# RWKV attention and a gated feed-forward network on one core: the first two chunks of two batches in 64-row half tiles of token pairs

## The chip, the core and the metric

The kernel runs on one core of a Trainium2 chip. It uses TensorE (PE in the profile; PEld is its weight loads), VectorE (DVE), ScalarE (ACT), GpSimd (POOL) and the DMA queues that SyncE (SP) and GpSimd issue. The metric is device time in microseconds, the median of several runs.

## What is computed

Inputs r, k, v, w are float32 of shape 4 batches x 8 heads x 768 tokens x 48. Each head keeps a 48x48 state; then a feed-forward network runs over all 3072 tokens, 384 wide, with 1536 units between:

```python
for t in range(S):
    cur = np.einsum('bhd,bhe->bhde', u[None] * kt, vt)
    y[:, :, t] = np.einsum('bhd,bhde->bhe', rt, state + cur)
    state = wt[:, :, :, None] * state + np.einsum('bhd,bhe->bhde', kt, vt)
...
x = y.transpose(0, 2, 1, 3).reshape(B * S, H * D)
xn = x / np.sqrt(np.mean(x * x, -1, keepdims=True) + 1e-6) * rms_g
g = xn @ w_gate
return (g / (1 + np.exp(-g)) * (xn @ w_val)) @ w_out
```

## The kernel before

The tokens of a batch are cut into 6 chunks of 128. A step is written `name.n.j`, for chunk n (0 to 5) of batch j (0 to 3). For each chunk:

- `load_r`, `load_k`, `load_v`, `load_w` (lines 256 to 271): a tile of 128 tokens by 8 heads by 48, in pieces of 192 bytes, because a head's row of one token is 48 floats. For the chunks in `WIN` (chunks 0 and 1 of each batch) one load of w brings 256 tokens, two tokens to a partition, in pieces of 384 bytes.
- `ln` (ACT) and `cs_mm` (PE): the logarithm of w and its running sums over the tokens, by matmuls with triangular masks. `exp_r`, `exp_k` (ACT) give the decays, `r_mul` (DVE) and `k_mul` (DVE or POOL) the decayed r and k, `w_tot` (DVE) the chunk's total decay.
- `rk_pe`, `rk_tr`: r and k are transposed, by PE and a copy in chunks 0 and 1, by a DMA transpose in later ones.
- `q_mm` (lines 493 to 504): the scores of a chunk, four pairs of heads, 48 rows by 128x128, even heads and odd heads in two banks. `q_mask_e`, `q_mask_o` mask them on DVE (or ACT and POOL).
- `st_mm`, `st_new`: the state's update. `y_mm` (lines 540 to 549): scores times v, 8 matmuls, and from chunk 1 on r times state, 4 matmuls.
- `bonus_mul`, `bonus_v` (POOL) and `bonus_sum` (DVE): the term with u. `x_add` (DVE) adds it to y; `x_sq`, `x_rstd`, `xn_mul` are the norm; `xn_pe` and `xn_out` (or a DMA transpose and `xn_gain`) give the transposed input of the network.

The network works on groups of 512 tokens (4 chunks). The table `COL` makes group 0 of chunks 0 and 1 of batches 0 and 1, and group 1 of those of batches 2 and 3. A group has 12 units of 128 columns: `gate_mm`, `val_mm` (line 617: three matmuls of 512 columns each; line 622: group 1, whose 512 tokens are done in two halves), `silu` (ACT), `h_mul` (DVE); then `o_mm` (line 660) for each chunk, `o_out` and `out_dma`. The weights come by `load_gv.g.h`: g 0 is the first 4 units, g 1 the other 8; h 0 is gate, h 1 value. `load_wo` brings the last matrix.

The order of all steps is written out by hand in the string `ORDER` (lines 25 to 126). Each engine takes its instructions in that order, SP its loads and POOL its weight loads too. PSUM has two banks in ring a, two in ring b and four in ring q. A step with `:m` in the table first does m filler matmuls with a tile of zeros into its bank (lines 235 to 241; three transposes for one filler where the bank is bfloat16). Sets such as `CAST_ACT`, `K_POOL`, `RK_DVE`, `ODD_DVE`, `RSTD_ACT`, `OUT_DVE` say which engine does a step for which chunk.

Of the kernel before, what the change touches and what calls it, by code (L numbers as in the profile page):

```python
# [30 lines left out]
bonus_mul.1.0 q_mask_e.0.0 load_k.1.3 load_r.1.2 load_k.1.2 load_r.1.3 load_v.1.2 bonus_mul.0.1 load_w.2.1 load_w.2.0
load_v.1.3 load_w.2.3 q_mm.1.0:2 cs_mm.1.1 exp_r.1.1 exp_k.1.1 r_mul.0.1 k_mul.0.1 w_tot.0.1 q_mask_o.1.0
bonus_sum.1.0 load_gv.0.1 cast_v.0.1 load_r.2.0 bonus_sum.0.1 r_mul.1.1 load_w.2.2 rk_pe.0.1:2 ln.0.3 y_mm.0.0
rk_tr.0.1 st_mm.0.1:4 x_add.0.0 q_mask_e.1.0 st_new.0.1 cs_mm.0.3:3 bonus_v.0.1 cast_v.1.0 q_mm.0.1:1 y_mm.1.0
k_mul.1.1 bonus_v.1.0 cast_v.1.1 q_copy_o.0.1 x_sq.0.0 bonus_mul.1.1 load_r.2.1 x_add.1.0 exp_r.0.3 load_r.2.2
x_sq.1.0 load_r.2.3 load_k.2.0 q_mask_e.0.1 w_tot.1.1 rk_pe.1.1:1 rk_tr.1.1 q_mm.1.1:7 q_mask_o.1.1 load_gv.0.0
q_mask_o.0.1 y_mm.0.1:8 g_mm.0.0 bonus_sum.1.1 ln.0.2 x_rstd.1.0 xn_mul.1.0 x_rstd.0.0 xn_mul.0.0 exp_k.0.3
bonus_v.1.1 load_gv.1.0 q_mask_e.1.1 x_add.0.1 x_sq.0.1 x_rstd.0.1 y_mm.1.1 x_add.1.1 k_mul.0.3 xn_pe.1.0:2 xn_pe.0.0
cs_mm.0.2 g_out.0.0 xn_out.1.0 x_sq.1.1 xn_mul.0.1 xn_out.0.0 r_mul.0.3 st_mm.1.1:3 x_rstd.1.1 st_mm.1.0 xn_mul.1.1
xn_pe.0.1 xn_out.0.1 w_tot.0.3 rk_pe.0.3:3 xn_pe.1.1 xn_out.1.1 exp_r.0.2 exp_k.0.2 r_mul.0.2 val_mm.0.0:4 gate_mm.0.3  # L40
silu.0.3 val_mm.0.3 rk_tr.0.3 w_tot.0.2 st_new.1.1 load_gv.1.1 k_mul.0.2 bonus_mul.0.2 q_mm.0.3 h_mul.0.3 st_new.1.0
gate_mm.0.2 gate_mm.0.0 rk_pe.0.2 silu.0.0 silu.0.2 val_mm.0.2 q_mask_e.0.3 h_mul.0.0 gate_mm.0.5 gate_mm.0.1 silu.0.5
silu.0.1 val_mm.0.1 rk_tr.0.2 q_copy_o.0.3 h_mul.0.1 bonus_mul.0.3 bonus_sum.0.3 h_mul.0.2 gate_mm.0.6:1
gate_mm.0.11:1 q_mm.0.2 cast_v.0.2 silu.0.6 silu.0.11 q_mask_o.0.2 gate_mm.0.8 val_mm.0.6 q_mask_e.0.2 cast_v.0.3
st_mm.0.2 val_mm.0.11 q_mask_o.0.3 h_mul.0.6 val_mm.0.5 y_mm.0.3 y_mm.0.2 bonus_sum.0.2 bonus_v.0.2 load_wo.0.0
# [668 lines left out]
```

## Time and profile before

| | |
|---|---|
| runs (3) | 203.38, 205.18, 205.36 us, median 205.18 |
| span of the profiled execution | 202.2 us; its own time isn't listed apart, the lowest run is 1.2 us above the span |
| first matmul of group 0 | 30.21 us |
| DMA, SP's queue | 119504 packets, 28.58 MB |

The page gives the busy time and share of each engine and a row of digits, each for a fortieth of the span (9 is 90% or more busy). In a timeline a row is the start, the length, the engine, the source line, the operation and its tiles, the number of instructions in it, and in brackets how long the engine stood idle before and what released it. Matmuls overlap: the time that one takes from the next is read from start to start.

### The profile page before, as it was taken

What the parts mean: (1) busy time and instruction counts of PE and PEld (TensorE: products, weight loads), DVE (VectorE), ACT (ScalarE), POOL (GpSimd) and SP (SyncE); (2) the same over time, 40 slices, a digit from 0 to 9 for tenths busy, and PEclk for the clock granted to TensorE, in tenths of its full rate; (3) what the DMA queues carried; (4) which work ended last, traced back from release to release, by engine and by line L of the source; (5) the groups of instructions that cost most, each with busy time, mean ns of one, the idle gap of its engine ahead of it and who ended that gap; (6) DMA issues with size and microseconds to landing.
All of it is one profiled execution on the core that took longest, in us unless ns stands there. A gap on an engine that the chain in (4) does not pass through costs nothing.

```text
span 202.2 us, 4604 instructions
## 1 busy us (share of the span) xinstructions
PE 191.3 (95%) x1677; PEld 121.9 (60%) x1694; DVE 157.5 (78%) x307; ACT 135.0 (67%) x278; POOL 124.4 (62%) x178
## 2 busy tenths in 40 slices
PE   1999799999999999999999998999999999999993
PEld 0566485565568998865556664656555555555562
DVE  6489789799989799997999998988989782225711
ACT  2637885779699657898678985899676683335310
POOL 6488959175769962689858556988699554200000
PEclk9999999999999999999999999999999999999999
DMA  6999999999999998989899999995464013030132
GB/s 144 231 234 207 212 208 202 195 179 208 206 184 225 160 212 191 210 185 188 199 176 215 237 188 203 183 190 108 134 179 104 0 23 99 0 117 0 63 115 99
DMA packets 121567, 32.42 MB, mean 160 GB/s; under 512 B 116420, under 2 KB 120392, under 8 KB 121544
## 3 DMA queue, kind: packets, MB, share of 16 engines
q1 hardware_dynamic: 119504, 28.58, 66.6%
q0 software_dynamic: 2032, 3.54, 9.9%
q8 instruction: 13, 0.21, 0.4%
q14 instruction: 10, 0.08, 0.1%
q10 hardware_dynamic: 8, 0.00, 0.0%
HBM read 25.96 MB, written 4.72 MB: 152 GB/s over the span
## 4 chain that ended last, share of the span: by engine, by line
PE 65%; ACT 3%; DMA 2%; DVE 2%; issue 1%; SPq 0%; DVEq 0%; ACTq 0%
PE ps_av L617 7%; PE ps_bu L617 7%; PE ps_au L617 7%; PE ps_bv L617 6%; PE ps_qx L660 6%; PE ps_qv L660 6%; PE ps_qu L660 5%; PE ps_qz L660 4%; PE ps_au L622 2%; PE ps_bu L622 2%; DMA rkT<-rk 2%; PE ps_av L622 2%; PE ps_bv L622 2%; ACT L249 1%; PE ps_au L419 1%; PE ps_qv L500 1%
## 5 line engine op out<-in xcount | busy, mean ns | idle before, releaser
L660 PEld LDWEIGHTS <-ht 128*128 128x128 bf16 x300 | 28.1, 98 | 17.5 <-DVE ht L646 1.0
L251 ACT ACTIVATE sg<-ps_av 128x512 bf16<-128x512 f32 x36 | 21.5, 597 | 22.8 <-PE ps_av L617 18.0
L646 DVE TENSOR_TENSOR ht<-ps_bv,sg 128x512 bf16<-128x512 f32 x29 | 19.9, 687 | 13.9 <-PE ps_bv L617 12.9
L251 ACT ACTIVATE sg<-ps_au 128x512 bf16<-128x512 f32 x36 | 21.5, 596 | 11.5 <-PE ps_au L617 7.7
L617 PEld LDWEIGHTS <-wg_sb 128*128 128x128 bf16 x180 | 19.2, 114 | 15.9 <-issue 0.6
L617 PEld LDWEIGHTS <-wv_sb 128*128 128x128 bf16 x180 | 19.2, 114 | 15.7 <-issue 0.5
L465 POOL TENSOR_TENSOR ruk<-rt,kt 128x384 f32<-128x384 f32 x24 | 24.0, 1001 | 3.7 <-DMA kt<-in_k_dram 2.8
L475 POOL TENSOR_TENSOR ydiag<-vt,diag 128x384 f32<-128x384 f32 x24 | 20.4, 859 | 9.4 <-DVE diag L470 9.1
L617 PE MATMUL ps_av<-xnt,wg_sb 128*128 128x512 bf16 x88 | 25.0, 381 | 0.3
L466 POOL TENSOR_TENSOR ruk<-ruk,u_bc 128x384 f32<-128x384 f32 x24 | 24.0, 1001 | 1.9
L617 PE MATMUL ps_bu<-xnt,wv_sb 128*128 128x512 bf16 x86 | 24.8, 380 | 0.4
L646 DVE TENSOR_TENSOR ht<-ps_bu,sg 128x512 bf16<-128x512 f32 x31 | 21.3, 686 | 4.8 <-PE ps_bu L617 3.1
L617 PE MATMUL ps_au<-xnt,wg_sb 128*128 128x512 bf16 x87 | 23.6, 380 | 0.1
L617 PE MATMUL ps_bv<-xnt,wv_sb 128*128 128x512 bf16 x82 | 23.2, 380 | 0.2
L459 POOL TENSOR_TENSOR rk<-kt,ek 128x384 bf16<-128x384 f32 x16 | 15.9, 1001 | 9.7 <-ACT ek L251 5.9
L249 ACT ACT_TABLE_LOAD x14 | 18.0, 1283 | 1.9 <-PEq L698 1.6
L660 PE MATMUL ps_qx<-wo_sb,ht 128*128 128x384 bf16 x96 | 17.1, 326 | 0.2 <-DVE ht L646 0.2
L558 ACT ACTIVATE junk<-xb 128x384 bf16<-128x384 f32 x24 | 12.5, 522 | 6.3 <-DVE xb L553 6.2
L571 ACT ACTIVATE xn<-xb,rstd 128x384 bf16<-128x384 f32 x24 | 14.2, 609 | 0.6 <-POOL rstd L567 0.5
L470 DVE TENSOR_REDUCE diag<-ruk 128x8 f32<-128x384 f32 x24 | 13.1, 544 | 1.9 <-POOL ruk L466 1.9
L660 PE MATMUL ps_qv<-wo_sb,ht 128*128 128x384 bf16 (+1 forms) x84 | 13.8, 314 | 0.0
L251 ACT ACTIVATE lw<-wt 128x384 bf16<-128x384 f32 (+1 forms) x20 | 11.6, 583 | 2.8 <-DMA wt<-in_w_dram 2.7
(170 smaller groups left out, 408.2 us busy)
## 6 DMA issues: line engine op xcount, KB each, us to landing
rt<-in_r_dram SPq DMA_DIRECT2D x24, 192.0 KB, 4.0
vt<-in_v_dram SPq DMA_DIRECT2D x24, 192.0 KB, 3.9
kt<-in_k_dram SPq DMA_DIRECT2D x24, 192.0 KB, 3.9
out_dram<-ob SPq DMA_DIRECT2D x23, 192.0 KB, 2.2
wt<-in_w_dram SPq DMA_DIRECT2D x16, 192.0 KB, 3.7
wt<-in_w_dram SPq DMA_DIRECT2D x4, 384.0 KB, 4.3
wo_sb<-in_moe_w_out_dram POOLq DMA_DIRECT2D x3, 384.0 KB, 7.3
wg_sb<-in_moe_w_gate_dram POOLq DMA_DIRECT2D x1, 768.0 KB, 9.2
```

What stands on the lines that cost most here:

```text
L249: nc.scalar.preload_act_table_set(table_name)
L251: return nc.scalar.activation(**kw).ins
L459: eng.tensor_tensor(out=rk[:, n % 2, j, 1, :, 0:D], in0=inp["k", n, j], in1=bank["cs_k", n, j][:, 0:DM].rearrange("p (h d) -> p h d", h=H) ...
L465: nc.gpsimd.tensor_tensor(out=ruk[n, j], in0=inp["r", n, j], in1=inp["k", n, j], op=ALU.mult)
L466: nc.gpsimd.tensor_tensor(out=ruk[n, j], in0=ruk[n, j], in1=u_bc, op=ALU.mult)
L470: nc.vector.tensor_reduce(out=diag[n, j].rearrange("p h o -> p (h o)"), in_=ruk[n, j], axis=mybir.AxisListType.X, op=ALU.add)
L475: nc.gpsimd.tensor_tensor(out=ydiag[n, j], in0=inp["v", n, j], in1=diag[n, j].to_broadcast([128, H, D]), op=ALU.mult)
L571: nc.scalar.activation(out=xn, in_=xb[n, j], func=AF.Copy, scale=rstd[n, j][:, 1:2])
L617: nc.tensor.matmul(ps, lhsT=units(ws, c, f), rhs=x[:, c, :], start=(c == 0), stop=(c == KC - 1))
L622: nc.tensor.matmul(ps[:, i * TS // 2:(i + 1) * TS // 2], lhsT=units(ws, c, f + i), rhs=x[:, c, cols], start=(i == 0 and c == 0), stop=(i = ...
L646: nc.vector.tensor_tensor(out=ht[n][:, f, :], in0=v, in1=sg, op=ALU.mult)
L660: nc.tensor.matmul(ps[:, cols], lhsT=ht[n][:, f, b * L:(b + 1) * L], rhs=wo_sb[:, f, cols], start=(f == 0), stop=(f == FC - 1))
```

## The change

Chunks 0 and 1 of batches 0 and 1 (the set `PAIR`) are laid out anew. A tile now holds one chunk of both batches: partitions 0 to 63 batch 0, 64 to 127 batch 1, each partition two neighbouring tokens. So r, k, v and w of one batch and chunk come as a 64-partition load in pieces of 384 bytes. A step `name.n.0` now means the even tokens of both batches, and `name.n.1` the odd ones. The sums use new masks `mp`, the scores new masks `mq`. Scores are 64x64 blocks for a batch: `q_mm` does 16 matmuls with 64 output rows in place of 8, `y_mm` 32 on scores in place of 8 and 8 on the state in place of 4, `st_mm` 8 in place of 4. The pair tiles lie in buffers that `ht` and `wo` use later. An output tile of such a chunk is written by two DMAs. The other batches keep the old form (`WIN` is now batches 2 and 3).

The sets that give steps to engines change, the order of all steps is new, and the new table has no filler. At its start it reads

```diff
-load_r.0.0 load_w.0.0 u_mm.0.0 ln.0.0 load_v.0.0 load_k.0.0 cs_mm.0.0:2 load_r.1.0 load_w.0.1 u_out.0.0 load_k.1.0
+u_mm.0.0 load_w.0.1 load_w.0.0 load_k.0.1 load_r.0.1 u_out.0.0 ln.0.0 cs_mm.0.0 load_w.1.0 load_r.0.0 load_k.0.0
```

The core of the rest:

```diff
-    CAST_ACT = sel("00 01 02 03 20 21 30 31 33 40 43 53")
+    CAST_ACT = sel("00 01 10 12 20 22 23 40 41 50 51 52 53")
-    K_POOL = sel("02 10 20 21 22 23 30 31 32 33 40 42 43 50 51 53")
+    K_POOL = sel("01 02 11 13 20 22 23 30 31 33 40 41 42 43 50 51 52")
-    WIN = sel("00 01 02 03 10 11 12 13")
+    WIN = sel("02 03 12 13")
+    PAIR = sel("00 01 10 11")
-    RK_DVE = sel("00 02 03 10 11 12 13")
-    ODD_DVE = sel("00 02 10 11 13 20 23 40 43 52")
-    RSTD_ACT = sel("00 10 11 13 20 32 33")
-    OUT_DVE = sel("00 01 10 13 20 21 22 30 33 40 42 50 52 53")
+    RK_DVE = sel("01 02 03 12 13")
+    ODD_DVE = sel("00 01 03 10 11 20 22 32 33 43 51")
+    RSTD_ACT = sel("00 01 03 11 12 13 21 43")
+    OUT_DVE = sel("00 03 11 22 31 40 42 50")
...
     def load(which, n, j):
         t = {"r": r, "k": k, "v": v}[which]
+        if (n, j) in PAIR:
+            if which == "v":
+                if "pv" not in inp:
+                    inp["pv"] = pt.tile([128, 2, H, 2, D], FP32, name="wo", bufs=1)
+                o = inp["pv"][:, n]
+            else:
+                if "prk" not in inp:
+                    inp["prk"] = pt.tile([128, 2, 2, H, 2, D], FP32, name="ht", bufs=NHT)
+                o = inp["prk"][:, n, "rk".index(which)]
+            b = j % 2
+            nc.sync.dma_start(out=o[b * PD:(b + 1) * PD].rearrange("p h i d -> p h (i d)"),
+                              in_=t[j, :, n * L:(n + 1) * L, :].rearrange("h (p i) d -> p h (i d)", i=2))
+            return
...
     def cs_mm(n, j):
+        if (n, j) in PAIR:
...
+            for x in range(2):
+                nc.tensor.matmul(o, lhsT=mp[:, int(x < i)], rhs=lw[:, n % 2, j0 + x, :, 0:D], start=(x == 0),
+                                 stop=(i == 1 and x == 1))
+            for q in range(0 if i else NP):
+                for x in range(2):
+                    nc.tensor.matmul(a[:, 2 * q:2 * q + 2], lhsT=pair(lw[:, n % 2, j0 + x], q), rhs=hb,
+                                     start=False, stop=(q == NP - 1 and x == 1))
...
     def q_mm(n, j):
+        if (n, j) in PAIR:
+            t, x = inp["rkT"][:, n], j % 2
...
+            for i in range(NP):
+                for b in range(2):
+                    at_b = slice(b * PD, (b + 1) * PD)
+                    for d0, o in ((0, qe), (PD, qo)):
+                        nc.tensor.matmul(o[at_b, i, :].rearrange("p (a x) -> p a x", a=2), lhsT=t[d0:d0 + D, NP + i, x, at_b],
+                                         rhs=t[d0:d0 + D, i, :, at_b], start=(i == 0), stop=(i == NP - 1))
...
     def y_mm(n, j):
+        if (n, j) in PAIR:
...
+            for h in range(H):
+                for s in range(2):
+                    for b in range(2):
+                        nc.tensor.matmul(ps[halves[b], h * D:(h + 1) * D],
+                                         lhsT=qts[n, j0 + s][halves[b], h % 2, h // 2, x * PD:(x + 1) * PD],
+                                         rhs=vb[n, j0 + s][halves[b], h, :], start=(n == 0 and h == 0 and s == 0),
+                                         stop=(h == H - 1 and s == 1))
...
     def out_dma(n, j):
+        if (i, j) in PAIR:
+            for b in range(2):
+                row0 = (j - j % 2 + b) * S + i * L
+                nc.sync.dma_start(out=out[row0:row0 + L].rearrange("(p a) m -> a p m", a=2)[j % 2],
+                                  in_=bank[ob][b * PD:(b + 1) * PD])
+            return
```

Three places of the order bear on the prediction. On PE, the last rows ahead of group 0. Before (L528 is `st_mm`, L586 `xn_pe`, L238 and L240 fillers, L482 `rk_pe`, L617 the network):

```order
L528 MATMUL ps_qu<-vb,rk 128x96
...
L586 MATMUL ps_qz<-ident,xn 128x128
...
L238 MATMUL ps_qv<-ident,zero 128x128
...
L482 MATMUL ps_qv<-ident,rk 128x128
...
L240 LDWEIGHTS zero
L240 MATMUL ps_bv<-zero 128x384
...
L617 LDWEIGHTS wv_sb_128
L617 MATMUL ps_bv<-xnt,wv_sb_128 128x512
```

The same place now (L711 is `xn_pe`, L633 `st_mm`, L553 `rk_pe`, L742 the network):

```order
L711 MATMUL ps_qv<-ident,xn 128x128
...
L633 LDWEIGHTS rk
L633 MATMUL ps_qu<-vb,rk 128x96
...
L553 LDWEIGHTS rk
L553 MATMUL ps_qv<-ident,rk 128x128
L742 LDWEIGHTS wg_sb_142
L742 MATMUL ps_au<-xnt,wg_sb_142 128x512
```

The fillers are gone, group 0 begins with a gate unit of the 8-unit part (`wg_sb_142`) where it began with a value unit of the 4-unit part (`wv_sb_128`), and `rk_pe` of both (0, 3) and (0, 2) stands ahead of it.

On POOL, the steps around the weight loads. Before (L465 and L466 are `bonus_mul`, L475 `bonus_v`, L389 `cast_v`, L351 the weights, L518 a mask, L566 and L567 `x_rstd`):

```order
L465 TENSOR_TENSOR ruk<-rt,kt 128x384
L466 TENSOR_TENSOR ruk<-ruk,u_bc 128x384
L351 DMA wv_sb_128<-in_moe_w_val_dram 128x3x512
L475 TENSOR_TENSOR ydiag<-vt,diag 128x384
L389 CAST vb<-vt 128x384
...
L351 DMA wg_sb_126<-in_moe_w_gate_dram 128x3x512
L518 AFFINE_SELECT qts<-qts 128x512
...
L351 DMA wg_sb_127<-in_moe_w_gate_dram 128x3x1024
L566 TENSOR_SCALAR rstd<-rstd 128x1
L567 TENSOR_TENSOR rstd<-rstd,mhalf 128x1
L351 DMA wv_sb_129<-in_moe_w_val_dram 128x3x1024
```

Now (L546 is `bonus_v`, L536 and L537 `bonus_mul.1.0`, L395 the weights, L435 `cast_v`, L530 `k_mul`, L691 and L692 `x_rstd`):

```order
L546 TENSOR_TENSOR ydiag<-wo,diag 128x384
L536 TENSOR_TENSOR ruk<-ht 128x384
L537 TENSOR_TENSOR ruk<-ruk,u_bc 128x384
L395 DMA wg_sb_142<-in_moe_w_gate_dram 128x3x1024
L395 DMA wv_sb_144<-in_moe_w_val_dram 128x3x1024
L435 CAST vb<-wo 128x384
L546 TENSOR_TENSOR ydiag<-wo,diag 128x384 x3
L530 TENSOR_TENSOR rk<-kt,ek 128x8x48
L691 TENSOR_SCALAR rstd<-rstd 128x1
L692 TENSOR_TENSOR rstd<-rstd,mhalf 128x1
L395 DMA wg_sb_141<-in_moe_w_gate_dram 128x3x512
L395 DMA wv_sb_143<-in_moe_w_val_dram 128x3x512
```

The two large weight loads now come first, behind all four `bonus_mul` and one `bonus_v`, and the small ones last.

On PE, the scores and `y_mm` of the first chunk, one matmul of each kind. Before:

```order
L500 LDWEIGHTS rkT
L500 MATMUL ps_qz<-rkT 128x128
L502 LDWEIGHTS rkT
L502 MATMUL ps_qu<-rkT 128x128
...
L548 LDWEIGHTS qts
L548 MATMUL ps_qz<-vb,qts 128x48
```

Now:

```order
L583 LDWEIGHTS ht
L583 MATMUL ps_qz<-ht 64x128
...
L583 MATMUL ps_qu<-ht 64x128
...
L662 LDWEIGHTS qts
L662 MATMUL ps_qu<-vb,qts 64x48
```

The outputs have 64 rows in place of 128, and there are 16 and 32 such matmuls in a step where there were 8 and 8.

More of the change, by code (lines that the diff above doesn't have):

```diff
@@ L31 @@
[L31 to L45, printed above, removed]
@@ new lines @@
+w_tot.1.3 r_mul.1.3 val_mm.0.1 gate_mm.0.0 silu.0.0 val_mm.0.2 y_mm.0.3 rk_pe.1.2 h_mul.0.2 gate_mm.0.1 silu.0.1
+val_mm.0.0 gate_mm.0.3 gate_mm.0.6 x_add.0.3 load_wo.0.0 k_mul.1.3 load_wo.1.0 x_rstd.0.2 load_wo.2.0 st_new.0.3
+h_mul.0.1 silu.0.3 x_sq.0.3 rk_tr.1.2 h_mul.0.0 xn_mul.0.2 silu.0.6 rk_pe.1.3 val_mm.0.3 q_mm.1.2 load_r.2.2 rk_tr.1.3
+cs_mm.2.1 val_mm.0.6 bonus_mul.1.2 bonus_mul.1.3 q_mask_e.1.2 h_mul.0.3 h_mul.0.6 cs_mm.2.0 q_mm.1.3 q_copy_o.1.2
+cast_v.1.2 x_rstd.0.3 q_mask_o.1.2 o_mm.0.2 bonus_sum.1.2 y_mm.1.2 bonus_v.1.2 q_mask_e.1.3 cs_add.2.0 ln.2.2
@@ L212, in banks_of @@
         }
+        if fn == "w_tot" and (n, j) in PAIR:
+            j -= j % 2
         return [(x, n, j) for x in found.get(fn, ())]
```

303 lines of the change are left out of this document (198 added, 105 removed).

## The prediction

> **What bounds the kernel now.** I read the page first, then the busy time by stretches, then the timeline of the first 30 us, and last the waits. Of the page, the totals, PE's row of the 40 slices and DMA's row:
>
> ```profile
> span 202.2 us, 4604 instructions
> ...
> PE 191.3 (95%) x1677; PEld 121.9 (60%) x1694; DVE 157.5 (78%) x307; ACT 135.0 (67%) x278; POOL 124.4 (62%) x178
> ...
> PE   1999799999999999999999998999999999999993
> ...
> DMA  6999999999999998989899999995464013030132
> ```
>
> PE is busy 95% of the span and the DMA engines are full for three quarters of it. The average hides two stages, so the next view cuts the span where the first matmul of the second network starts (the last columns are granted clock, DMA share and GB/s):
>
> ```profile
> 7.93:30.16 22.23, 20.44 (x269) 14.49 (x268) 18.49 (x40) 15.41 (x37) 17.58 (x23) 1.00 1.13 221
> 30.21:199.01 168.80, 167.02 (x1394) 105.72 (x1409) 135.04 (x256) 116.91 (x239) 102.63 (x141) 1.00 0.73 153
> ```
>
> From 30.21 us on, PE is idle 168.80 - 167.02 = 1.8 us in 169: the long stretch is PE's work and almost nothing else. Before it, in what I call the head, PE looks full too, but 70 of its matmuls there and just behind it are fillers with zeros (the counts on `zero`):
>
> ```profile
> L240 PEld LDWEIGHTS <-zero 128*128 128x128 bf16 x40 | 3.5, 98 | 2.8 <-issue 1.1
> ...
> L238 PEld LDWEIGHTS <-zero 128*128 128x128 bf16 x30 | 2.2, 107 | 0.5 <-issue 0.3
> ...
> 22.97 1.47 PE L240 MATMUL ps_qv<-zero 128*128 128x384 bf16 x8
> ```
>
> So the head is paced by others: DVE is busy 18.49 of 22.23 us, POOL 17.58. It ends with this chain, from the last chunk's sum through its norm and transpose to the first matmul of group 0:
>
> ```profile
> 7.93 0.56 DVE L453 TENSOR_TENSOR rk<-rt,ps_au 128x384 bf16<-128x384 f32 x1 [1.54 <-ACT ps_au L251]
> ...
> 25.92 0.56 DVE L553 TENSOR_TENSOR xb<-ps_qx,ydiag 128x384 f32<-128x384 f32 x1 [0.30 <-PE ps_qx L548]
> ...
> 28.50 0.62 ACT L571 ACTIVATE xn<-xb,rstd 128x384 bf16<-128x384 f32 x1
> ...
> 29.60 0.56 DVE L596 TENSOR_TENSOR xnt<-ps_qz,gT 128x384 bf16<-128x384 bf16 x1 [0.43 <-PE ps_qz L586]
> ...
> 30.21 0.81 PE L617 MATMUL ps_bv<-xnt,wv_sb 128*128 128x512 bf16 x2
> ```
>
> The time is therefore the moment of that first matmul, plus PE's work behind it, plus PE's stalls behind it, plus a tail of 3.2 us (202.2 - 199.0) that the change leaves alone.
>
> **The change, part by part.** *PE's work behind the first matmul.* The order shows the same 360 + 144 + 300 matmuls of the second network there, with the same shapes, and the same attention steps but two: the eight transposes of `rk_pe.0.2` are now ahead of it, and two fillers are gone. The eight transposes take 0.44 us from start to start:
>
> ```profile
> 28.79 0.61 PE L482 MATMUL ps_qv<-ident,rk 128*128 128x128 bf16 x8
> ...
> 29.23 0.33 PE L586 MATMUL ps_qz<-ident,xn 128*128 128x128 bf16 x3
> ...
> 36.94 0.33 PE L240 MATMUL ps_av<-zero 128*128 128x384 bf16 x1
> ...
> 37.10 0.81 PE L617 MATMUL ps_av<-xnt,wg_sb 128*128 128x512 bf16 x3
> ```
>
> A filler takes 0.16 us. Together -0.44 - 0.32 = **-0.8 us**. The fillers of the head cost nothing when they go (they are some 40 x 0.16 + 30 x 0.055 = 8 us of PE, put in front of waits), unless the clock needs them; that is a rival below.
>
> *Loads.* Twelve loads of r, k and v change from 1024 packets of 192 bytes to 512 of 384. One stretch with the first kind alone and one with mostly the second:
>
> ```profile
> 2.00:3.00 1.00, 0.00 (x0) 0.00 (x0) 0.91 (x1) 0.92 (x1) 0.86 (x4) 1.00 0.99 203
> 11.00:12.00 1.00, 1.00 (x14) 0.47 (x12) 1.00 (x5) 0.00 (x0) 1.00 (x2) 1.00 1.15 312
> ```
>
> A load has 196.6 KB: 0.97 us at 203 GB/s, 0.63 at 312, or 0.72 if 312 is scaled by the shares (0.99/1.15). Twelve save 12 x 0.25 to 0.34 = 3 to 4 us of DMA time. That is a gain only where something waits for a load. But a step now needs both batches' loads: `k_mul.0.0` waits for the seventh half-tile load. Packets start at 2.0 us, 7 x 0.70 us follow, and landing adds 0.8: 7.7 us, no earlier than now, where the first product on POOL starts at 7.08. What does come earlier is w, loaded first: two loads, 2.0 + 1.4 + 1.0 = 4.4 us against 5.42. PE's own first matmul waits for the ones row, which is now made ahead of the widest mask and not behind it, so it isn't in the way:
>
> ```profile
> 4.16 1.64 PE L372 MATMUL ps_qu<-u_bc,ones_row 1*128 1x384 f32 x2 [4.16 <-POOL ones_row L338]
> ...
> 5.42 0.84 ACT L251 ACTIVATE lw<-wt 128x768 bf16<-128x768 f32 x1 [2.50 <-DMA wt<-in_w_dram]
> ...
> 7.08 1.00 POOL L465 TENSOR_TENSOR ruk<-rt,kt 128x384 f32<-128x384 f32 x1 [2.84 <-DMA kt<-in_k_dram]
> ```
>
> So DVE's first step of the head moves from 7.93 with w to about 7.0 us.
>
> *DVE and POOL in the head.* From the first product to the last `xn_out` DVE has 39 steps now and 40 after (one r product, one mask and one `w_tot` more; one k product and one copy of transposes less), so its work stays the same within half a us. POOL has two k products there for one, one cast for two, and no mask. The spacing of both, from start to start where they run back to back, and POOL's two other steps:
>
> ```profile
> 11.86 1.00 POOL L465 TENSOR_TENSOR ruk<-rt,kt 128x384 f32<-128x384 f32 x1
> ...
> 12.94 1.00 POOL L466 TENSOR_TENSOR ruk<-ruk,u_bc 128x384 f32<-128x384 f32 x1
> ...
> 17.66 0.55 DVE L553 TENSOR_TENSOR xb<-ps_qz,ydiag 128x384 f32<-128x384 f32 x1
> ...
> 18.12 0.68 DVE L507 TENSOR_TENSOR qts<-ps_qx,mask_lt 128x512 bf16<-128x512 f32 x1
> ...
> 18.72 0.55 DVE L535 TENSOR_TENSOR st<-ps_qu,wcol 128x384 bf16<-128x384 f32 x1
> ...
> L475 POOL TENSOR_TENSOR ydiag<-vt,diag 128x384 f32<-128x384 f32 x24 | 20.4, 859 | 9.4 <-DVE diag L470 9.1 <-DVE wcol L449 0.3
> ...
> L389 POOL CAST vb<-vt 128x384 bf16<-128x384 f32 x12 | 6.0, 503 | 4.4 <-DMA vt<-in_v_dram 4.4
> ```
>
> That is 1.08 us a POOL product, 0.46 us a DVE step of 0.55 and 0.60 a mask. I followed the new orders by hand with these. POOL starts at 7.7, does ten products and a `bonus_v` (10 x 1.08 + 0.86 = 11.7 us), and issues the two large weight loads at 19.4 and 20.3 us; then one cast and three `bonus_v` (0.5 + 3 x 0.94) end at 24.6. DVE waits for `bonus_v.0.1` at 22.7 and for `bonus_v.1.0` at 24.6, so `x_add.1.1` starts at 25.1, against 25.92 now. From there the present chain takes 30.21 - 25.92 = 4.3 us; the new one has `rk_tr.0.3` ahead of the last `xn_out` on DVE, but that fits in the wait for the norm, and I count 4.0. First matmul: 29.1 us by the walk. A walk by hand leaves out small waits; DVE's idle 3.7 us of the head came from such. So I take 29.6, between 29.1 and the present 30.2: **-0.6 us**.
>
> *The 64x64 matmuls.* In the two chunks `q_mm` has 16 matmuls a step for 8 and `y_mm` 32 small ones for 8 (and 8 for 4 on the state):
>
> ```profile
> 18.73 0.23 PE L500 MATMUL ps_qv<-rkT 48*128 48x128 bf16 x1
> ...
> 18.91 0.22 PE L500 MATMUL ps_qv<-rkT 48*128 48x128 bf16 x1
> ...
> 58.12 0.20 PE ps_qx L548 x8
> ```
>
> Two scores now run side by side every 0.06 us and eight small matmuls take 0.20, 25 ns each. For a `y_mm` of 32 that bounds the cost between 0.8 us and, at 55 ns each, 1.8 us; for `q_mm` between 0.23 and 0.9. I take the cheap end, because neighbours here too use different halves of the array, as the pairs of scores now do. Then the four `y_mm` and their like add some 3 us to PE, in place of the fillers. Only the last two `y_mm` stand on the chain, and there DVE waits for POOL until 24.6 us anyway; at the dear end they end 1.4 us too late for it. [...]
>
> *Buffers and outputs.* The pair tiles lie in the buffers of `ht` and `wo`. Their last readers are `bonus_v.1.0` and `y_mm.1.1`, done by 26 us, and the next users (`h_mul`, `load_wo`) come behind the first matmul, so I cost that at nothing. Four more issues of outputs on SP stand between loads that are due tens of us later: nothing, too; if a load behind them is late after all, it is one of the stalls below.
>
> *Stalls behind the head.* All orders are new. PE's idle time there is 1.8 us; the new order can win at most that, and can lose more. Taking -1.8 and +4 as the ends, I choose **+1.0**.
>
> Sum: -0.6 - 0.8 + 1.0 = -0.4, a span of 201.8. The profiled span of 202.2 lies 1.2 us below the lowest of the three runs (203.38) and 3.0 below their median of 205.18; I set the difference against the median: **204.8 us**.
>
> **Rivals.** *The clock (slower).* Now the clock is low until about 10 us: two 384-wide matmuls take 0.84 us at first and 0.50 later, 0.16 more for each, which is half speed (the clock column of the stretches shows 1.00 there all the same; I go by the durations):
>
> ```profile
> 7.84 0.84 PE L404 MATMUL ps_av<-lw,mw 128*128 128x384 bf16 x2
> ...
> 11.80 0.50 PE L404 MATMUL ps_au<-lw,mw 128*128 128x384 bf16 x2
> ```
>
> PE began at 4.16, so it needed nearly 6 us of work to rise. Without fillers PE has about 2 us of work in the last 5 us ahead of group 0. If the clock falls there, 6 us of matmuls at half speed lose 3 us, and slow steps in the head up to 1 more: 207.8 to 208.8. For it: 8 of PE's 20 us in that stretch were fillers. Against it: the longest hole in my walk is 1.5 us. [...] It decides if PE's granted speed is still half at the first matmul of group 0.
>
> *The weights (slower).* Group 0 now begins with units of the second, 8-unit part, so PE waits for the large loads:
>
> ```profile
> 25.35 0.80 POOL L351 DMA_DIRECT2D wg_sb<-in_moe_w_gate_dram  x1
> ...
> wg_sb<-in_moe_w_gate_dram POOLq DMA_DIRECT2D x1, 768.0 KB, 9.2
> wv_sb<-in_moe_w_val_dram POOLq DMA_DIRECT2D x1, 768.0 KB, 11.5
> ```
>
> Issued at 19.4 and 20.3, they land at 28.6 and 31.8; first use is at 29.6 and some 3 us later. Once POOL is more than 1 us late, each further us costs one; at 3 to 4 us late, which the DMA queues in front of its first products could make, that is +2 to +3: 206.8 to 207.8.
>
> *The 64x64 tiles at the dear end (no change).* +1.4: 206.2.
>
> *Faster.* The walk holds to the letter (29.1) and the new order also wins 1.0 of the 1.8 us of stalls: -1.1 - 0.8 - 1.0 = -2.9: 202.3. For it: 3.7 us of idle DVE in the head; against it: POOL, which the change does not relieve.
>
> **Chances.** Forecast 0.32 (its own range 203.3 to 206.8), clock 0.28, faster 0.20, weights 0.12, dear tiles 0.08. One per cent, 2.05 us, is about what a measurement can tell from no change. Faster by more: 0.17 of the faster rival and 0.03 of the forecast, 0.20; slower: 0.22 of the clock, 0.08 of the weights, 0.03 of the forecast, 0.33; within: 0.47. The range for 8 in 10 takes in most of the faster rival and of the clock: 202.0 to 208.8.
>
> **What would show it.** The first matmul of group 0 near 29.6 us; 32 `y_mm` matmuls in under 1 us; 384-wide matmuls at 0.16 us apart from 12 us on; POOL's weight issues near 19.4 and 20.3 us; PE idle behind the head under 3 us. I am wrong where group 0 starts at half speed, where PE waits for `wg_sb`, or where one of the later groups shows a new hole of several us.

## The result, and the profile after

The changed kernel takes 216.75 us (median of 4 runs, 215.21 to 217.73), the kernel before 204.36 in the runs beside it: a ratio of 1.062, 95% interval 1.057 to 1.067. The prediction was 204.8 us, with 202.0 to 208.8 as its range. Runs over 1.5% above the fastest of their kernel, among them one of 401.45 us of the ten in experiment 4, count in the medians below but not in most of the ratios, so a ratio can differ from the quotient of two medians. The profiled execution took 217.14 us. Four rows of its page, the span, PE's and the clock's row and DMA's row of the 40 slices (5.4 us each):

```profile
span 215.3 us, 4767 instructions
...
PE   3778834999999999999997999999999999899993
PEclk9999655599999999999999999999999999999999
DMA  5999999999990398979999999986276203100042
```

Slices 6 and 7 of PE show a hole that the kernel before hasn't got, and the granted clock is near half from slice 5 to 8. The next view gives busy times by stretches: the last 16.7 us ahead of group 0, and the stretch behind its first matmul (columns as in the prediction).

```profile
23.62:40.32 16.70, 10.05 (x139) 7.43 (x138) 7.60 (x17) 7.93 (x19) 7.43 (x10) 0.50 1.06 194
40.32:211.80 171.48, 168.60 (x1402) 105.98 (x1400) 130.81 (x248) 118.06 (x244) 99.96 (x137) 0.99 0.68 141
```

The first matmul of group 0 comes at 40.32 us in place of 30.21: 10.1 of the span's 13.1 us are lost in the head. The stretch behind it has 171.48 us for 168.80: 2.7 more. The tail has 0.3 more. In the first stretch all five engines are busy less than two thirds of the time: they wait for each other in a row, and behind a load. The timeline of the head says which (rows of POOL, DVE and PE, in order of time):

```profile
9.82 1.00 POOL L536 TENSOR_TENSOR ruk<-ht 128x384 f32<-128x384 f32 x1 [3.27 <-DMA ht<-in_k_dram]
...
20.63 0.98 POOL L395 DMA_DIRECT2D wg_sb<-in_moe_w_gate_dram  x1
21.62 0.79 POOL L395 DMA_DIRECT2D wv_sb<-in_moe_w_val_dram  x1
...
34.36 0.56 DVE L524 TENSOR_TENSOR rk<-rt,ps_au 128x384 bf16<-128x384 f32 x1 [7.93 <-DMA rt<-in_r_dram]
...
35.30 0.55 DVE L678 TENSOR_TENSOR xb<-ps_qu,ydiag 128x384 f32<-128x384 f32 x1
35.44 0.48 PE L711 MATMUL ps_qv<-ident,xn 128*128 128x128 bf16 x3 [6.50 <-DVE xb L678]
...
40.32 1.49 PE L742 MATMUL ps_au<-xnt,wg_sb 128*128 128x512 bf16 x3
```

DVE stands still for 7.93 us before `r_mul.0.3`, the r product of chunk 0 of batch 3, because that chunk's r hasn't landed. It isn't needed yet: it serves group 1. But it stands in DVE's order ahead of `x_add.1.0` and `x_add.1.1`, on which the norm, the transposes and group 0 hang, so all of them wait with it.

Why is a load so late that SP began to issue by 23 us? SP's own rows (issues and how long SP was held), and the DMA queues in a stretch of that wait (q0 holds POOL's weight loads, q1 SP's; packets, MB, share of 16 engines):

```profile
19.78 3.33 SPq L281 DMA_DIRECT2D rt<-in_r_dram  x2
23.16 7.03 SPq L281 DMA_DIRECT2D kt<-in_k_dram  x1
```

```profile
q0 software_dynamic: 278, 0.54, 94.9%
q1 hardware_dynamic: 279, 0.05, 16.2%
```

Between 27 and 30 us both queues moved the same number of packets, 278 and 279. But a packet of the weights has 2048 bytes and one of SP's loads 192, so SP's queue got 0.05 of 0.59 MB. A load that wasn't done when the 1.5 MB of weights began lay nearly still until they were through: POOL's queue moved 143 packets between 30 and 32 us and 5 in the 2 us behind them, and the r product ran at 34.36. In the kernel before, POOL issued two loads of half that size at 16.63 and 23.15 us and the two large ones only at 25.35 and 27.36; SP issued the same r from 18.17 us on, and the r products at 28.08 and 30.07 had no wait. So two questions stand: why was r only being issued when the weights began at 20.6 us (SP held its two issues from 19.78 to 23.11), and how much of the loss is this wait, how much the clock, how much the rest?

### The profile page after: what moved, and what is told of

It is laid out like the page before. It is cut to its first block, busy times and chain, and to the rows that moved or that the text cites. A ratio compares the mean times of both kernels' runs of the same rounds, so it can differ in the third digit from the quotient of the medians.

```text
span 215.3 us, 4767 instructions
## 1 busy us (share of the span) xinstructions
PE 194.3 (90%) x1760; PEld 123.1 (57%) x1760; DVE 153.1 (71%) x300; ACT 140.2 (65%) x288; POOL 125.7 (58%) x181
## 4 chain that ended last, share of the span: by engine, by line
PE 56%; DMA 15%; POOL 8%; ACT 6%; SPq 6%; issue 5%; DVE 2%; POOLq 0%; DVEq 0%; ACTq 0%
PE ps_au L742 7%; PE ps_av L742 7%; PE ps_bu L742 7%; PE ps_bv L742 6%; DMA rt<-in_r_dram 6%; DMA rkT<-rk 4%; PE ps_qv L785 4%; PE ps_qu L785 3%; PE ps_qz L785 3%; DMA wt<-in_w_dram 2%; SPq L281 2%; POOL ruk L536 2%; SPq L277 2%; ACT junk L683 2%; PE ps_qx L785 2%
## 5 line engine op out<-in xcount | busy, mean ns | idle before, releaser
L254 ACT ACTIVATE sg<-ps_av 128x512 bf16<-128x512 f32 x37 | 22.1, 598 | 13.1 <-PE ps_av L742 11.1
L771 DVE TENSOR_TENSOR ht<-ps_bv,sg 128x512 bf16<-128x512 f32 x28 | 19.2, 687 | 14.7 <-ACT sg L254 11.0
L742 PEld LDWEIGHTS <-wg_sb 128*128 128x128 bf16 x180 | 19.5, 116 | 17.1 <-issue 1.6
L742 PEld LDWEIGHTS <-wv_sb 128*128 128x128 bf16 x180 | 19.4, 114 | 16.5 <-issue 0.8
L742 PE MATMUL ps_bu<-xnt,wv_sb 128*128 128x512 bf16 x96 | 26.0, 380 | 0.0
L742 PE MATMUL ps_av<-xnt,wg_sb 128*128 128x512 bf16 x93 | 25.9, 389 | 0.0
L537 POOL TENSOR_TENSOR ruk<-ruk,u_bc 128x384 f32<-128x384 f32 x24 | 24.5, 1020 | 1.9
L742 PE MATMUL ps_au<-xnt,wg_sb 128*128 128x512 bf16 x87 | 24.5, 392 | 0.0
L742 PE MATMUL ps_bv<-xnt,wv_sb 128*128 128x512 bf16 x84 | 22.7, 379 | 0.6 <-POOL xnt L727 0.6
L546 POOL TENSOR_TENSOR ydiag<-vt,diag 128x384 f32<-128x384 f32 x20 | 16.7, 843 | 9.7 <-DVE diag L541 7.9
L536 POOL TENSOR_TENSOR ruk<-rt,kt 128x384 f32<-128x384 f32 x20 | 20.1, 1003 | 0.2
L683 ACT ACTIVATE junk<-xb 128x384 bf16<-128x384 f32 x24 | 12.4, 518 | 10.2 <-DVE xb L678 10.1
L691 POOL TENSOR_SCALAR rstd<-rstd 128x1 f32<-128x1 f32 x16 | 3.1, 191 | 25.9 <-ACT junk L683 25.3
L530 POOL TENSOR_TENSOR rk<-kt,ek 128x384 bf16<-128x384 f32 x15 | 15.2, 1023 | 3.3 <-ACT ek L254 3.3
L785 PE MATMUL ps_qv<-wo,ht 128*128 128x384 bf16 (+1 forms) x96 | 15.0, 306 | 0.0
L785 PE MATMUL ps_qu<-wo,ht 128*128 128x384 bf16 x84 | 14.8, 326 | 0.0
```

Source lines behind the costliest of these rows:

```text
L254: return nc.scalar.activation(**kw).ins
L530: eng.tensor_tensor(out=rk[:, n % 2, j, 1, :, 0:D], in0=arr("k", n, j), in1=bank["cs_k", n, j][:, 0:DM].rearrange("p (h d) -> p h d", h=H) ...
L536: nc.gpsimd.tensor_tensor(out=ruk[n, j], in0=arr("r", n, j), in1=arr("k", n, j), op=ALU.mult)
L537: nc.gpsimd.tensor_tensor(out=ruk[n, j], in0=ruk[n, j], in1=u_bc, op=ALU.mult)
L546: nc.gpsimd.tensor_tensor(out=ydiag[n, j], in0=arr("v", n, j), in1=diag[n, j].to_broadcast([128, H, D]), op=ALU.mult)
L683: nc.scalar.activation(out=junk, in_=xb[n, j], func=AF.Square, accum_out=rstd[n, j][:, 0:1])
```

## The experiments

Times stand beside the kernel before in the same group of runs (203.5 to 204.4 us). Theory A: the weight loads keep r from landing, and that blocks DVE. Rival B: the clock. Rival C: the new order's small stalls. The first four runs:

**1. The weights later.**

```diff
-load_gv.1.0 load_gv.1.1        (ahead of cast_v.1.1)
+load_gv.1.0 load_gv.1.1        (behind bonus_v.1.0)
```

> The changed kernel with one edit: POOL issues the two 768-KB weight loads (gate and value, second part) behind the four bonus_v of the pairs, at about 25 us in place of 20.6; SP's own list of loads is untouched. Theory A (the weight loads take the DMA engines from the load of r of chunk 0 of batch 3, which then blocks DVE and the last two x_add behind it): that load lands by about 26 us, DVE's wait of 7.9 us is nearly gone, the first matmul of group 0 comes at 32 to 33 us in place of 40.3, and the time falls by 6 to 9 us, to 208 to 211. Rival B (the clock, which fell at 23.6 us before any long wait, is the main loss): the clock still falls, and the time stays at 214 or more. Rival C (the new order and the pair layout lose the time in small stalls everywhere): under 2 us gained.

Measured: 210.59 us, ratio 1.034 (1.025 to 1.042). DVE's wait is gone, the row has no bracket; now PE waits for the weights themselves:

```profile
27.84 0.54 DVE L524 TENSOR_TENSOR rk<-rt,ps_au 128x384 bf16<-128x384 f32 x1
```

```profile
36.99 0.61 PE L742 MATMUL ps_au<-xnt,wg_sb 128*128 128x512 bf16 x1 [2.08 <-DMA wg_sb<-in_moe_w_gate_dram]
```

That is 6.2 us under the changed kernel's median (5.7 by the ratios), at the lower end of what A says. The moment isn't as expected: the first matmul came at 37, not 33. The `bonus_v` ended so late that the weights were issued at 27.4 us, and DVE was at other work until 27.84: the head is late even without the wait.

**2. The waiting step later.**

```diff
-r_mul.0.3 ... w_tot.0.3 ... r_mul.0.2 ... rk_pe.0.3 ... rk_pe.0.2   (ahead of the last xn_out)
+r_mul.0.3 w_tot.0.3 gate_mm.0.7 r_mul.0.2 w_tot.0.2 gate_mm.0.4 rk_pe.0.3 rk_tr.0.3 rk_pe.0.2 rk_tr.0.2   (behind it)
```

> The changed kernel with the loads as they are, but the r products, the w_tot and the transposes of chunk 0 of batches 2 and 3 put behind the last xn_out, and the first two gate_mm among them. The late load then blocks nothing ahead of the norm. Theory A: the last two x_add come at 26.5 to 28.5 us in place of 34.8 and 35.3; the first gate_mm still needs the bank that the r product reads, so it comes at about 35.2 in place of 40.3; gain 4 to 6 us, 211 to 213. Rival B (clock): the first matmuls of group 0 run at half speed all the same, longer than now, and the gain is under 2 us. Rival C: under 1 us.

Measured: 213.6 us, ratio 1.045 (1.037 to 1.052).

```profile
34.89 0.58 PE L742 MATMUL ps_au<-xnt,wg_sb 128*128 128x512 bf16 x1 [1.98 <-DVE wcol L519]
```

The first `gate_mm` came at 34.89 as worked out: it takes the bank that the late product reads. The gain is 3 us by the medians, 4.1 between the two profiled executions, for 5.4 us of head; where the rest went (the blocked work is now done between PE's units) wasn't traced. A holds, with a gain under its range.

**3. Fillers for the hole.**

```diff
-xn_pe.1.0
+xn_pe.1.0:44
```

> The changed kernel with 44 x 3 filler transposes on PE ahead of the transposes of xn of chunk 1 of batch 0, that is, in the hole of 6.5 us; nothing else. Theory A: the wait for r stays, the first matmul of group 0 stays at 40 us or comes up to 1 us earlier, and only the 1.9 us that group 0 loses at half speed come back: 214 to 215.5. Rival B (the clock carries the loss): 206 to 210.

Measured: 221.39 us, ratio 1.085. The experiment missed its aim. The step on which PE waits is `xn_pe.0.1`, whose bank is held until the late `x_add`; it stands ahead of `xn_pe.1.0` in PE's order. So the fillers ran behind the wait, which ended at 35.39 us, not in it, and held PE for 8.7 us more:

```profile
35.39 0.48 PE L711 MATMUL ps_qv<-ident,xn 128*128 128x128 bf16 x3 [7.62 <-DVE xb L678]
...
37.41 8.84 PE L241 MATMUL ps_qv<-ident,zero 128*128 128x128 bf16 x132
...
47.53 0.81 PE L742 MATMUL ps_au<-xnt,wg_sb 128*128 128x512 bf16 x2
```

It says nothing on the clock. Behind the step that waits, these fillers weren't free.

**4. The kernel before without its fillers.** All `:m` taken out.

> The kernel before with all its fillers taken out, order and layout as they were. It prices the fillers by themselves. If the clock needs them (the changed kernel without them had full speed only from 16.8 to 23.6 us ahead of group 0): the clock falls in the head, the first matmuls of group 0 run at half speed, and the time rises by 2 to 5 us, to 206.5 to 209.5. If they are only waste in waits: 203.5 to 204.5, no difference.

Measured: 204.99 against 203.57 us, ratio 1.005 (1.001 to 1.009). The granted clock fell in the head (slices 5 and 6 of the page; two 384-wide matmuls took 0.80 us at 28.03 and 0.48 at 43.45), and by the ratio the missing fillers cost 0.9 us, not 2 to 5:

```profile
PEclk9999859999999999999999999999999999999999
```

Here rival B is real but small. Group 0 began at full speed in this kernel (0.81 us for three 512-wide matmuls at 32.26), so the price of a slow start of group 0 isn't in it; experiments 5, 6 and 11 give that.

**5. The shape of the pair loads.** The r, k and v loads of the pairs, and their w loads likewise:

```diff
-            nc.sync.dma_start(out=o[b * PD:(b + 1) * PD].rearrange("p h i d -> p h (i d)"),
-                              in_=t[j, :, n * L:(n + 1) * L, :].rearrange("h (p i) d -> p h (i d)", i=2))
+            nc.sync.dma_start(out=o[:, 4 * b:4 * b + 4].rearrange("p h i d -> p h (i d)"),
+                              in_=t[j - b, 4 * b:4 * b + 4, n * L:(n + 2) * L, :].rearrange("h (p i) d -> p h (i d)", i=2))
```

> The changed kernel with other shapes of the pair loads: each of the 16 loads still brings 512 pieces of 384 bytes, but four heads of 256 tokens of one batch into all 128 partitions, in place of eight heads of 128 tokens into 64 partitions. It computes with other tokens than it should in chunks 0 and 1 of batches 0 and 1; the work is the same. Theory D (a load into 64 partitions gets its pieces through slower, so the head's loads come late): a 384-byte piece takes 22 to 24 ns in place of 32 to 35, POOL's first product starts at 7.5 to 8.5 us in place of 9.82, and the load of r of chunk 0 of batch 3 is 2 to 3 us nearer to landing when the weights begin, so DVE's wait falls to 0 to 5 us and the time by 4 to 10 us. If the pieces take as long as before, the number of partitions has nothing to do with it, and the time stays within 1 us of 216.7.

This kernel reads other tokens than it should in the pairs and can't be used; its work is the same. Measured: 204.79 us, ratio 1.005 (1.002 to 1.009): 12 us come back, more than the 4 to 10 expected, from loads of the same bytes and the same pieces that fill 128 partitions in place of 64. SP's queue between 6 and 12 us, in the changed kernel and in this one:

```profile
q1 hardware_dynamic: 3571, 1.33, 130.0%
```

```profile
q1 hardware_dynamic: 4817, 1.80, 111.8%
```

Worked out as share x 16 engines x 6 us by packets, a piece took 34.9 ns and now 22.3; a load of 196.6 KB 0.89 us and now 0.66. The head then runs nearly as the prediction walked it (rows of SP, POOL, DVE and PE):

```profile
8.38 1.00 POOL L536 TENSOR_TENSOR ruk<-ht 128x384 f32<-128x384 f32 x1 [1.84 <-DVE rk L524]
...
17.10 1.58 SPq L281 DMA_DIRECT2D rt<-in_r_dram  x2
...
19.21 0.98 POOL L395 DMA_DIRECT2D wg_sb<-in_moe_w_gate_dram  x1
20.20 0.79 POOL L395 DMA_DIRECT2D wv_sb<-in_moe_w_val_dram  x1
...
24.23 0.54 DVE L524 TENSOR_TENSOR rk<-rt,ps_au 128x384 bf16<-128x384 f32 x1
...
25.17 0.54 DVE L678 TENSOR_TENSOR xb<-ps_qu,ydiag 128x384 f32<-128x384 f32 x1
...
30.18 1.49 PE L742 MATMUL ps_au<-xnt,wg_sb 128*128 128x512 bf16 x3
```

`r_mul.0.3` waits for nothing, although the weights are issued even earlier: SP was through with the issues of r at 18.68, ahead of the weights, where the changed kernel was at them until 23.11. So theory A's wait is the end of a chain that begins with dear loads. This is theory D, and it holds. It also bounds the clock: PE was at half speed from 20 us into group 0 here too (the first three gate matmuls took 1.49 us; 0.81 at full speed), and still the 12 us came back.

**6. The late weights with fillers** (46 in 19 steps of the head, such as `cs_mm.1.1:6`, `xn_pe.0.1:4`).

> The kernel with the late weights (210.6 us) and 46 fillers, spread over 19 steps of PE in the head where it waits for others. Rival B (the clock costs the head several us): full speed from 12 us on, the matmuls on the chain take 0.16 in place of 0.32 us, and the time falls by 3 to 5 us, to 206 to 207.5. Theory A (PE is not on the chain in the head, only the first matmuls of group 0 are slow for want of the clock): 1 to 2.5 us less, 208 to 209.5. Fillers that stand in the way of the chain: no gain or a loss.

Measured: 209.09 us, ratio 1.026 (1.023 to 1.029): 1.5 us less than without, at a granted clock of 1.0 over the profiled run for 0.956. That is A's range, not B's. But not A's reason: the first matmul of group 0 came at 35.01 us for 36.99, so the head was 2 us shorter as well.

**7 and 8. Small weights first, r ahead of w of chunk 2; and with fillers.** Units 0 to 3 take the places of 7, 4, 11 and 5 in group 0's order.

```diff
-load_w.2.0 load_v.1.1 load_k.0.2 load_k.0.3 ... load_gv.1.0 load_gv.1.1 ... load_r.0.2 load_r.0.3
+load_r.0.3 load_r.0.2 load_v.1.1 load_k.0.2 load_k.0.3 load_w.2.0 ... load_gv.0.0 load_gv.0.1 ... load_gv.1.0 load_gv.1.1
```

> The changed kernel with all that theory A asks for: group 0 begins with the four units of the first, small part (384 KB a weight) in place of four of the large part; these two loads are issued where the large ones were, at 20.6 us, the large ones behind the fourth bonus_v; the loads of r of chunk 0 of batches 2 and 3 come ahead of the load of w of chunk 2, whose logarithm moves behind the norm. Theory A: no step of the head waits over 1 us for a load of r, the first matmul of group 0 comes at 31.5 to 34 us, and the time is 206.5 to 209.5. Rival C (small stalls of the new order): 211 or more.

> The kernel just named, with the 46 fillers. Theory A: another 1 to 2.5 us less, 205 to 207.5, still not under the kernel before, since its loads of the head land 2 us later. Rival B: 3 to 5 us less, 203 to 205.

Measured: 209.16 us (ratio 1.026, 1.023 to 1.030), and 211.71 with fillers (1.039, 1.034 to 1.044; its four runs are 208.25, 211.03, 212.40 and 215.87, so the step from 7 to 8 isn't settled, and the gain that was expected of the fillers didn't come). In the first of the two the head has no wait for r of batches 2 and 3, and the first matmul of group 0 comes earlier:

```profile
32.66 1.49 PE L742 MATMUL ps_au<-xnt,wg_sb 128*128 128x512 bf16 x3
```

32.66 us lies in A's 31.5 to 34. But 5 us of the 12 remain: with the loads dear, this order alone doesn't mend it.

**9 and 10. A queue for each half; and with fillers.**

```diff
+            (nc.sync if b else nc.scalar).dma_start(...)     (pair loads; those of batch 0 on ACT's queue)
```

The order of the loads is changed too, so that ACT issues its share earlier.

> The changed kernel, correct layout, 64-partition loads of 384-byte pieces as they are; but the eight loads of batch 0's halves (partitions 0 to 63) are issued by ACT on its own queue, those of batch 1's halves (64 to 127) stay with SP, so that a load into each half is under way at the same time. Theory D1 (a load into 64 partitions uses half of the paths into the memory, and the other half stands idle): the two loads fill both, a piece takes 22 to 28 ns with both queues at work, the loads of r of chunk 0 of batches 2 and 3 land before the weights, and the time is 205 to 209, with ACT's issues (8 of 0.6 us) as a cost. Theory D2 (such a load is slow by itself, for instance because each piece of 64 partitions costs more work wherever it goes): pieces stay at 32 to 35 ns or slower, and the time stays over 212.

> The kernel with two queues and the 46 fillers. If the clock is held through the head: 1 to 2.5 us under the kernel without fillers, 203.5 to 207. Beating the kernel before (203.8) by 1 per cent would need the first matmul of group 0 under 28.5 us; I give that a small chance.

Measured: 210.48 us (ratio 1.032, 1.026 to 1.037) and 208.05 (1.016, 1.008 to 1.025). The second has the lowest ratio of the kernels of this layout with its own tokens, though its interval overlaps with that of experiment 6. The two queues' rows between 6 and 12 us in the first give 28.3 ns a piece ((0.775 + 0.306) x 16 x 6000 / 3670), near D1's range; but the time lies between the two, because ACT issues behind its own work (its load of k of chunk 0 stands behind the logarithm in the order), so that k came late, POOL waited 4.93 us for it and began later than ever, at 11.46. That leaves D1 likely and not shown:

```profile
q1 hardware_dynamic: 2523, 0.95, 77.5%
q10 hardware_dynamic: 1147, 0.43, 30.6%
```

```profile
11.46 1.00 POOL L536 TENSOR_TENSOR ruk<-ht 128x384 f32<-128x384 f32 x1 [4.93 <-DMA ht<-in_k_dram]
```

**11. Full-height loads with fillers.** Edits 5 and 6 together.

> The kernel with the full-height pair loads (wrong tokens in the pairs, same work; 204.8 us) and the 46 fillers. In it the clock was at half from 19.4 to 33.1 us. With the clock held, group 0's first 2.9 us are not slow and the head's last PE steps are short: 1.5 to 3 us less, 202 to 203.5. If the fillers stand in the way of the chain: 204 or more.

Measured: 203.61 us against 203.53, ratio 1.000 (0.996 to 1.003). The clock (1.0 granted over the profiled run for 0.966) is worth another 1.2 us here, a little under the range. With dear loads and clock out of the way, the new order and matmuls are as fast as the old: no faster. (It too reads the wrong tokens.)

**12. The loads by themselves.**

> Loads alone: this kernel leaves all of the computation out and writes zeros. It makes eight stages of eight loads of 196.6 KB each, one stage after the other: (1) 64 partitions 0 to 63, 384-byte pieces; (2) the same into partitions 32 to 95; (3) 128 partitions by four heads, 384 bytes; (4) in turn into 0 to 63 and 64 to 127, SP's queue; (5) the same, one half from SP's queue, the other from ACT's; (6) 128 partitions by eight heads, 192 bytes; (7) as 6, with a 768-KB weight load from POOL beside it; (8) as 3, with such a weight load. Theory D1 (half of the paths into the memory stand idle in a load to 0 to 63): stages 1 and 4 take 32 to 36 ns a piece and some 220 GB/s, stage 2 is as fast as stage 3 (22 to 24 ns, 290 to 310 GB/s), because 32 to 95 reaches both halves; stage 5 lies between. Theory D2 (64 partitions are slow wherever they lie): stage 2 is as slow as stage 1. Stages 7 and 8: if the DMA engines take one piece in turn from each queue, SP's queue moves as many pieces as the weights', so 192 bytes for each 2048 in 7 and 384 in 8 (about 16 and 30 KB per us); if they share by bytes, SP's queue keeps near half.

This kernel computes nothing, and ran once. Its stages, from the view by stretches (core, then DVE, POOL, clock, DMA share, GB/s): stages 1 to 6 in turn, and 7 and 8 while the weights are under way.

```profile
5.00:9.00 4.00, 0.58 (x4) 0.00 (x0) 1.00 1.30 201
14.00:18.00 4.00, 1.44 (x10) 0.00 (x0) 1.00 1.02 270
24.00:26.00 2.00, 0.31 (x2) 0.00 (x0) 1.00 1.09 294
31.00:35.00 4.00, 0.59 (x4) 0.00 (x0) 1.00 1.11 253
40.00:44.00 4.00, 0.59 (x4) 0.00 (x0) 1.00 1.25 257
48.00:53.00 5.00, 0.77 (x5) 0.00 (x0) 1.00 1.13 221
59.00:62.00 3.00, 0.00 (x0) 0.00 (x0) 1.00 1.11 191
73.00:76.00 3.00, 0.00 (x0) 0.00 (x0) 1.00 1.04 180
```

With the queue rows of stages 1, 2 and 3 a piece costs 38.7, 22.4 and 22.2 ns (the first: 1.304 x 16 x 4000 / 2155):

```profile
q1 hardware_dynamic: 2155, 0.80, 130.4%
...
q1 hardware_dynamic: 2898, 1.08, 101.6%
...
q1 hardware_dynamic: 1576, 0.59, 109.4%
```

Partitions 0 to 63: 201 GB/s. The same 64 partitions' worth at 32 to 95: 270. So here it wasn't the number of partitions but where they lie, as D1 expected of these two stages (38.7 and 22.4 ns a piece). That half of the paths stand idle, the reason D1 gives, no view shows. (Partitions 64 to 127 weren't run alone.) Note stage 6 too: 192-byte pieces into 128 partitions move 221 GB/s, more than the 201 of 384-byte pieces into the low half. What the longer pieces were to gain in the loads is lost again in the half.

Stage 4 was expected to be as slow as 1 and wasn't (253 GB/s, 26.1 ns), and stage 5, with a queue for each half, is hardly better (257). Why turns between the halves move more than the low half alone was not shown. Stages 7 and 8, weights beside:

```profile
q0 software_dynamic: 259, 0.53, 97.8%
q1 hardware_dynamic: 227, 0.04, 13.2%
...
q0 software_dynamic: 226, 0.46, 89.6%
q1 hardware_dynamic: 200, 0.08, 14.7%
```

Packets 259 to 227 and 226 to 200, whatever their size: some 13 and 27 KB per us for SP's queue, near the 16 and 30 expected of turns by pieces.

**13, 14 and 15. Halves in turn in the real kernel**; alone, on kernel 7, and with fillers.

```diff
-load_w.0.1 load_w.0.0 load_k.0.1 load_r.0.1 load_w.1.0 load_r.0.0 load_k.0.0 load_k.1.1 load_w.1.1 load_r.1.0 load_r.1.1 load_k.1.0
+load_w.0.1 load_w.0.0 load_k.0.1 load_r.0.0 load_r.0.1 load_k.0.0 load_w.1.1 load_w.1.0 load_r.1.1 load_r.1.0 load_k.1.1 load_k.1.0
```

The last v load of the pairs also moves ahead of w of chunk 2.

> The changed kernel, layout and result unchanged, with SP's first twelve pair loads in another order, so that loads into partitions 0 to 63 and 64 to 127 take turns (now up to three loads into the same half follow each other), and the last v pair load ahead of w of chunk 2. From the loads measured alone: the same half over and over 38.7 ns a piece, in turn 26 ns. If that holds here: 26 to 30 ns in place of 35 between 6 and 12 us, POOL's first product at 8.5 to 9.3 us in place of 9.82, the load of r that blocks DVE 1.5 to 2.5 us nearer to landing before the weights begin; the time 207 to 214, wide because the wait is all or little. If the order of the halves doesn't matter beside the other loads: 215 to 218.

> The kernel with the small weights first (209.2 us), with the same turns of halves. The head's loads come 1 to 2 us earlier: 206.5 to 208.5. If the head there is paced by DVE and POOL and not by its loads: 209.

> The kernel just named with the 46 fillers: the clock held, 204.5 to 207.5; below the kernel before (203.5) only if the first matmul of group 0 comes before 30 us, which the loads at 26 ns leave little room for.

Measured: 215.35 us (ratio 1.056, 1.049 to 1.063), 212.05 (1.031, 1.022 to 1.041) and 210.44 (1.029, 1.024 to 1.035). The first lies where the order of the halves doesn't matter, the others above all that was expected. The turns won nothing on kernel 7: the interval of 14 overlaps with that of 7, and its first matmul of group 0 came at 32.59 us for 32.66. The first of them, SP's queue between 6 and 12 us, POOL's rows, and DVE's wait:

```profile
q1 hardware_dynamic: 3821, 1.42, 126.7%
```

```profile
8.55 1.01 POOL L536 TENSOR_TENSOR ruk<-ht 128x384 f32<-128x384 f32 x1 [2.02 <-DMA ht<-in_k_dram]
...
19.50 0.98 POOL L395 DMA_DIRECT2D wg_sb<-in_moe_w_gate_dram  x1
```

```profile
DVE rk L524 <- DMA rt<-in_r_dram: 8.2, 1, 8.2
```

Between 6 and 12 us 1.42 MB came for 1.33, 31.8 ns a piece for 34.9 (26 to 30 were expected), and POOL began where expected. But POOL then reached its weights 1.1 us sooner too, caught r under way once more, and DVE waited 8.2 us. Here the faster front, not fast enough, only brought the weights forward. The turns don't mend the layout, and no kernel here beat the kernel before.

## Why the prediction was wrong, step by step

- **Loads: wrong, and this step carries the miss.** "0.97 us at 203 GB/s, 0.63 at 312, or 0.72" took the price of a 384-byte load from stretches in which such pieces went into all 128 partitions, and used it for loads into 64. Measured: 0.89 us where 0.70 stood. For the seventh load the walk said 7.7 us; POOL's first product came at 9.82. The lags that the walk added for landing (0.8 us, and 1.0 for w) were estimates, and no view shows them by themselves; if loads are moved in the order of issue, the packets of the changed kernel's queue give 1.0 us for w (two loads of 512 packets through at 4.0, `ln` at 5.04) and 1.5 for the seventh load (8.3 and 9.82). The term "twelve save 3 to 4 us" came to nothing: between 2 and 18 us SP's queue moved 3.65 MB here, 3.68 MB in the kernel before and 4.34 MB in experiment 5. And "a gain only where something waits for a load" was asked of the wrong loads: r of chunk 0 of batch 3, whose load lies behind sixteen such loads, wasn't in the walk.
- **The walk of the head: right, given the loads.** With full-height loads (experiment 5) the weight issues came at 19.21 and 20.20 (19.4 and 20.3), the last `x_add` at 25.17 (25.1), the first matmul at 30.18 (29.6), though the clock was at half. In part two errors cancel: POOL began at 8.38 (7.7), and its ten products and `bonus_v` took 10.8 us (11.7). In the changed kernel the first matmul came at 40.32.
- **What the walk left out.** It followed POOL and DVE and never asked whether each load of the head is through when the weights begin. The weights were treated as late arrivals (a rival), not as something that keeps others off. Nothing waited for them in the changed kernel; r waited because of them. That, with `r_mul.0.3` ahead of the two `x_add`, made loads that were 0.2 us dearer each than priced into 10 us of head.
- **PE's work behind the first matmul (-0.8) and stalls (+1.0): too dear by 1.1 together.** With loads and clock mended (experiment 11):

```profile
30.99:198.92 167.93, 166.49 (x1401) 105.63 (x1399) 130.32 (x248) 117.77 (x244) 99.54 (x137) 1.00 0.72 150
```

  That is 167.93 us for 168.80, so -0.9 for the two together where +0.2 was predicted: PE's busy time fell by 0.5, its idle time from 1.8 to 1.4. In the changed kernel the stretch was 2.7 longer: PE idle 2.9 us for 1.8, and the matmuls up to 44 us at half speed.
- **64x64 tiles: right, the cheap end.** Cheaper even, 32 in 0.69 us (0.8 was the lower end), and their weight loads in 0.58:

```profile
20.27 0.58 PEld L662 LDWEIGHTS <-qts 64*64 64x64 bf16 x32
...
20.27 0.69 PE L662 MATMUL ps_qu<-vb,qts 64*64 64x48 bf16 x32
```

  The dear end, 55 ns each and 1.8 us, is out. By the view of lines a weight load of these 32 lasted 109 ns in the mean; one behind the other they would take 3.5 us and not 0.58, so they overlapped.
- **Rival clock: its condition came true, its price did not.** PE was at half speed at the first matmul (three 512-wide matmuls in 1.49 us at 40.32, where experiment 11 has 0.81). But by itself the clock is worth 0.9 to 1.5 us (experiments 4, 6 and 11), not 3 to 4.
- **Rival faster: out.** Experiment 11 comes nearest to what the forecast describes (loads at the price assumed, full clock, though by fillers), and it ends at the kernel before, ratio 0.996 to 1.003. That its sum agrees with the forecast of -0.4 us is luck: the first matmul came at 30.99 us, 0.8 later than before where 0.6 earlier was forecast, and the stretch behind it made that good.
- **Buffers and outputs at nothing:** the waits of the changed kernel show 0.9 us in which DVE waited for an output buffer, for 1.6 in the kernel before, and none for the buffers of the pairs; not tested alone.

## What to carry to other kernels

Take the price of a load from a row with the same partitions, not only the same piece size: loads into one half of the partitions each took 1.35 times as long in the changed kernel as full ones in experiment 5 (0.89 by 0.66 us), and 1.46 times as long alone (294 by 201 GB/s). Before a large load on another queue is issued, list every load that is still under way and who stands behind its reader: here two queues moved about as many pieces each, and the one with small pieces all but stopped (0.05 of 0.59 MB in 3 us). A step that needs a late load and isn't urgent belongs behind the urgent ones on its engine, and where it can, the urgent chain shouldn't need its bank either.
